# Re-packing a convolution's output through DRAM, half a super ahead of its use, in a fused convolution and two-matmul kernel

## The chip, the cores and the metric

The kernel runs on one core of one Trainium2 chip. The metric is the time of one execution in device microseconds. A profile gives the span of one execution, which is about 2 us shorter than its time.

The core's engines are named as the profile names them: PE multiplies matrices (PEld is its loading of weights), ACT, DVE and POOL work element by element, and SP here only issues DMA transfers; a q after a name is that engine's instruction queue. SBUF is the memory on the core, PSUM the one that PE writes to. To evacuate is to copy a result out of PSUM. The granted clock is the share of PE's full clock that the chip allows at that time.

## The reference, cut to what matters

```python
# x: (8, 4096, 192); weight: (8 heads, 7 taps); w_in: (192, 2048); w_out: (2048, 192)
w   = softmax(weight, axis=-1)
att = causal_conv7(x, w)          # per head of 24 channels, 7 taps back in time
h   = att @ w_in                  # 32768 tokens x 2048
g   = where(h > 0, h, exp(min(h, 0)) - 1)
out = g @ w_out                   # 32768 x 192
```

## The kernel before

Tokens go in 32 "supers" of 1024. The work of one super is:

- **conv**: two convolutions (first and second 512 tokens), each 40 small matmuls into a PSUM slot, evacuated by ACT to `csb`. In a PSUM tile each head stands in a slot of 32 partitions, of which 24 are used.
- **re-pack**: the second matmul contracts over 192 channels in three chunks of 64 partitions, twice over (two row groups of PE). SP moves the rows from the slots to `att` with 20 copies inside SBUF.
- **16 pairs**: each pair is 12 matmuls `H<-att,w_in` into one of three PSUM slots, then exp on ACT, clamp on POOL, max on DVE, giving `gT`.
- **output rounds**: 64 rounds of 4 matmuls `ops<-w_out,gT` for each half of the super, dealt out between the pairs of the *next* super, from its pair 3 (`LAG`).

The order of PE, ACT and SP comes from one list:

```python
LAG = 3; NG3 = 3
HALF_STEPS = (10, 9, 9, 9, 9, 9, 9)     # output rounds per pair, for 7 pairs
CONV_AT = (2, 10)                       # convs of super s+1 after pairs 2 and 10 of super s
...
for n in range(NP + NQ + LAG + NQ):     # n = pair number, s = super, i = pair in the super
    s, i = divmod(n, NQ)
    if n < NP: order.append(("h", n))                   # H matmuls
    if n in rounds_at: order.append(("o",) + rounds_at[n])   # output rounds
    if i in CONV_AT and s + 1 < NS and n < NP: order.append(("c", 2*(s+1) + CONV_AT.index(i)))
```

PE, in a pair: wait for `att` of the super, wait for the PSUM slot, 12 matmuls.

```python
W(s_att, 16 * NDMA_ATT * (s + 1))
wait_slot(k)
for j in range(3):
    for r in range(2):
        for c in range(2):
            pe.matmul(H[HP*c:HP*(c+1), k % 3, GS*r:GS*(r+1)],
                      w_in[HP*r:HP*(r+1), j, HP*f:HP*(f+1)],
                      att[HP*r:HP*(r+1), s % 2, j, c, :], ...)
```

SP, when both convs of a super have been evacuated:

```python
W(s_ce, m + 1)
if s >= 2: W(s_h, NQ * (s - 1))
for (hb, sl, r0, nr, j, d0) in MOVES:          # 10 moves of 8 to 24 partitions
    for r in range(2):                         # once for each row group
        sy.dma_start(att[HP*r+d0 : HP*r+d0+nr, s % 2, j, :, :],
                     csb[SLOT*sl+r0 : SLOT*sl+r0+nr, s % 2, hb, :, :]).then_inc(s_att, 16)
```

POOL, besides its clamp, issues the loads of x for three supers ahead at pair 8 of each super: one strided load of eight windows, one for the ninth, and at the start of a batch (every fourth super) a memset and a third load.

## Time and profile before

| kernel before | |
|---|---|
| time | 1244.28 us, median of 4 runs (1237.9 to 1247.79) |
| span of the profiled run | 1240.6 us |
| mean granted PE clock | 0.863 |
| time from one super to the next | 37.6 us in the mean of 28 (36.7 to 38.8) |

The page's first part gives each engine's busy time (us, share of the span, number of instructions); part 4 gives the chain of work that ended last, as shares of the span.

```profile
span 1240.6 us, 55031 instructions
PE 818.5 (66%) x25088; PEld 594.9 (48%) x25088; DVE 666.7 (54%) x1043; ACT 656.3 (53%) x1156; POOL 666.4 (54%) x1120
...
SPq 35%; PE 30%; POOL 10%; DVE 8%; ACT 6%; DMA 6%; issue 4%; ACTq 0%; DVEq 0%
SPq L447 35%; PE H L398 16%; PE ops L418 13%; DVE gT L339 7%; POOL E L237 6%; DMA att<-csb 5%; ACT E L284 3%; ACT csb L273 3%; POOL xg L201 2%; PE H L376 2%; POOL xg L202 1%; DVE Ttmp L323 1%; ACT osb L260 0%; DVE Tm L327 0%; POOL xg L192 0%
```

No engine is busy two thirds of the time, and the largest part of the chain is SP issuing DMAs (line 447, the re-pack). The waits view of the same kernel says who stood still for it (total us, number of times, longest):

```profile
POOL E L237 <- ACT E L284: 552.9, 407, 26.4
DVE gT L339 <- POOL E L237: 533.7, 257, 22.1
ACT E L284 <- PE H L398: 525.5, 407, 17.6
PE H L398 <- DMA att<-csb: 312.7, 32, 17.2
```

The first three lines are one queue: POOL waits for ACT, DVE for POOL, ACT for PE. Only the last line names a cause: 32 supers, 32 waits of PE for the re-pack, about 10 us each. The timeline of one super shows how it comes about (start us, duration us, engine, line, what, count, and in brackets the idle time before it and what ended it):

```profile
615.73 1.02 ACT L273 ACTIVATE csb<-H 128x1024 bf16<-128x1024 f32 x1 [0.47 <-PE H L376]
616.78 15.81 SPq L447 DMA_DIRECT2D att<-csb  x20
...
621.89 0.82 PE L398 MATMUL H<-att,w_in 64*64 64x512 bf16 x12
622.54 0.91 PE L418 MATMUL ops<-w_out,gT 64*64 64x192 f16 x36
...
633.98 1.50 PE L398 MATMUL H<-att,w_in 64*64 64x512 bf16 x12 [10.53 <-DMA att<-csb]
```

The second conv is evacuated at 616.75, after pair 10. SP needs 15.1 us from the first of the 20 issues to the last (which starts at 631.87), and PE goes on 2.1 us after that. PE has work only until 623.4. The first pair after the gap then takes 1.50 us instead of 0.82. The windows view of the same kernel (us, busy time and count for each engine, granted PE clock, DMA share, GB/s) shows why:

```profile
617.00:622.00 5.00, 5.00 (x192) 4.11 (x188) 3.63 (x7) 3.89 (x8) 3.56 (x6) 1.00 0.30 78
623.00:634.00 11.00, 0.47 (x28) 0.26 (x16) 2.27 (x4) 0.85 (x2) 1.43 (x3) 0.73 0.20 48
634.00:637.00 3.00, 3.00 (x52) 2.17 (x56) 0.08 (x1) 1.08 (x2) 0.80 (x2) 0.50 0.00 0
```

Before the gap the granted clock is 1.00, after it 0.50. The Trainium skill (TensorE: Matmul & The Clock Gate, Part 1) tells of a clock gate that halves the clock when PE has been idle and opens only after about 3.4 us of activity; the 3 us window at 0.50 agrees in size.

### The profile page before, as it was taken

What the parts mean: (1) busy time and instruction counts of PE and PEld (TensorE: products, weight loads), DVE (VectorE), ACT (ScalarE), POOL (GpSimd) and SP (SyncE); (2) the same over time, 40 slices, a digit from 0 to 9 for tenths busy, and PEclk for the clock granted to TensorE, in tenths of its full rate; (3) what the DMA queues carried; (4) which work ended last, traced back from release to release, by engine and by line L of the source; (5) the groups of instructions that cost most, each with busy time, mean ns of one, the idle gap of its engine ahead of it and who ended that gap; (6) DMA issues with size and microseconds to landing.
All of it is one profiled execution on the core that took longest, in us unless ns stands there. A gap on an engine that the chain in (4) does not pass through costs nothing.

```text
span 1240.6 us, 55031 instructions
## 1 busy us (share of the span) xinstructions
PE 818.5 (66%) x25088; PEld 594.9 (48%) x25088; DVE 666.7 (54%) x1043; ACT 656.3 (53%) x1156; POOL 666.4 (54%) x1120
## 2 busy tenths in 40 slices
PE   0556666766568766668766578666678566577667
PEld 0234445544446545445544455454455454455446
DVE  4555456554456545556545466454566454565553
ACT  1655456554556554556545466554566455465543
POOL 4654456554556544566544566455566544565443
PEclk9988889888888887889888898888898888898879
DMA  9221323221232212232213232213232213221111
GB/s 159 37 47 39 67 55 62 58 47 53 59 64 59 58 38 64 56 66 58 58 37 67 55 63 57 58 41 67 56 62 59 50 49 67 56 58 47 38 50 54
DMA packets 97721, 71.20 MB, mean 57 GB/s; under 512 B 52048, under 2 KB 84816, under 8 KB 97488
## 3 DMA queue, kind: packets, MB, share of 16 engines
q1 hardware_dynamic: 54928, 50.40, 14.8%
q0 software_dynamic: 42560, 17.29, 12.6%
q8 instruction: 196, 3.21, 1.1%
q14 instruction: 37, 0.30, 0.1%
HBM read 34.59 MB, written 25.17 MB: 48 GB/s over the span
## 4 chain that ended last, share of the span: by engine, by line
SPq 35%; PE 30%; POOL 10%; DVE 8%; ACT 6%; DMA 6%; issue 4%; ACTq 0%; DVEq 0%
SPq L447 35%; PE H L398 16%; PE ops L418 13%; DVE gT L339 7%; POOL E L237 6%; DMA att<-csb 5%; ACT E L284 3%; ACT csb L273 3%; POOL xg L201 2%; PE H L376 2%; POOL xg L202 1%; DVE Ttmp L323 1%; ACT osb L260 0%; DVE Tm L327 0%; POOL xg L192 0%
## 5 line engine op out<-in xcount | busy, mean ns | idle before, releaser
L339 DVE SCALAR_TENSOR_TENSOR gT<-E,H 128x512 f16<-128x512 f32 x1024 | 651.4, 683 | 552.4 <-POOL E L237 533.7
L237 POOL TENSOR_SCALAR E<-E 128x512 f32<-128x512 f32 x1024 | 606.5, 615 | 553.8 <-ACT E L284 552.9
L284 ACT ACTIVATE E<-H 128x512 f32<-128x512 f32 x1024 | 557.0, 599 | 526.3 <-PE H L398 525.5
L398 PE MATMUL H<-att,w_in 64*64 64x512 bf16 x6144 | 470.2, 414 | 353.5 <-DMA att<-csb 312.7
L418 PEld LDWEIGHTS ops<-w_out,gT 64*64 64x64 f16 x16384 | 406.4, 115 | 107.4 <-issue 33.8
L418 PE MATMUL ops<-w_out,gT 64*64 64x192 f16 x16384 | 452.3, 256 | 4.0 <-issue 2.1
L398 PEld LDWEIGHTS H<-att,w_in 64*64 64x64 bf16 x6144 | 169.5, 115 | 445.2 <-DMA att<-csb 302.4
L273 ACT ACTIVATE csb<-H 128x1024 bf16<-128x1024 f32 x64 | 66.5, 1040 | 35.7 <-PE H L376 35.7
L376 PE MATMUL H<-Tm,xg 128*24 128x122 bf16 (+3 forms) x2560 | 41.6, 211 | 60.7 <-DVE gT L339 42.6
L376 PEld LDWEIGHTS H<-Tm,xg 128*24 128x24 bf16 x2560 | 32.9, 93 | 88.9 <-DVE gT L339 56.6
L260 ACT ACTIVATE osb<-ops 128x768 f32<-128x768 f32 x64 | 52.2, 816 | 16.8 <-PE ops L418 16.4
L201 POOL DMA_DIRECT2D xg<-in_x_dram x32 | 30.1, 941 | 0.4 <-issue 0.4
L202 POOL DMA_DIRECT2D xg<-in_x_dram x32 | 18.4, 575 | 0.0
L323 DVE TENSOR_TENSOR Ttmp<-shift,wprb 128x976 bf16<-128x976 bf16 x6 | 7.0, 1175 | 0.2
L192 POOL DMA_DIRECT2D xg<-in_x_dram x8 | 4.7, 590 | 0.0
L327 DVE TENSOR_TENSOR Tm<-Tm,Ttmp 128x976 bf16<-128x976 bf16 x6 | 4.0, 667 | 0.2
L210 POOL TENSOR_SCALAR_AFFINE_SELECT shift<-shift 128x122 bf16<-128x122 bf16 x7 | 2.7, 466 | 0.0
L295 DVE MEMSET H<- 128x2048 f32 x1 | 1.8, 1765 | 1.3 <-PEq L479 1.3
L225 POOL DMA_DIRECT2D w_out<-in_moe_w_out_dram x2 | 2.2, 1102 | 0.0
L191 POOL MEMSET xg<- 6x192 bf16 x8 | 2.0, 248 | 0.0
L249 ACT ACT_TABLE_LOAD x1 | 1.3, 1283 | 0.8 <-PEq L479 0.8
L220 POOL DMA_DIRECT2D w_in<-in_moe_w_in_dram x2 | 1.3, 644 | 0.0
(14 smaller groups left out, 4.4 us busy)
## 6 DMA issues: line engine op xcount, KB each, us to landing
out_dram<-osb SPq DMA_DIRECT2D x128, 192.0 KB, 3.1
att<-csb SPq DMA_DIRECT2D x384, 48.0 KB
xg<-in_x_dram POOLq DMA_DIRECT2D x24, 384.0 KB, 5.1
att<-csb SPq DMA_DIRECT2D x128, 32.0 KB
xg<-in_x_dram POOLq DMA_DIRECT2D x8, 336.0 KB, 4.8
att<-csb SPq DMA_DIRECT2D x128, 16.0 KB
xg<-in_x_dram POOLq DMA_DIRECT2D x32, 48.0 KB, 4.6
w_in<-in_moe_w_in_dram POOLq DMA_DIRECT2D x2, 768.0 KB, 8.1
```

Source lines behind the costliest of these rows:

```text
L201: g.dma_start(xg[:, b, w0:8, :], src).then_inc(s_x[b], 16)
L202: g.dma_start(xg[:, b, 8, :], x_flat[t0 + SUP - P : t0 + SUP, :]).then_inc(s_x[b], 16)
L237: g.tensor_scalar(out=E[:, n % NE, u, :], in0=E[:, n % NE, u, :], scalar1=1.0, scalar2=0.0, op0=ALU.min, op1=ALU.max,).then_inc(s_clp)
L260: a.activation(osb[:, b, :, :, :].rearrange("p g k d -> p g (k d)"), ops[:, :, 0 : 2 * D], ACT.Copy,).then_inc(s_oev)
L273: a.activation(csb[:, s % 2, :, g, :], H[:, slot_of_conv[m] % 3, :].rearrange("p (b t) -> p b t", b=2), ACT.Copy,).then_inc(s_ce)
L284: a.activation(E[:, n % NE, u, :], H[:, k, GS * u : GS * (u + 1)], ACT.Exp).then_inc(s_exp)
L323: v.tensor_tensor(dst[:, :, :], sd, wd, ALU.mult).then_inc(s_set)
L339: v.scalar_tensor_tensor(out=gT[:, s % NG3, 2 * q + u, :], in0=E[:, n % NE, u, :], scalar=1.0, in1=H[:, slot_of_pair[n] % 3, GS * u : GS * ...
L376: ins = pe.matmul(H[SLOT * q : SLOT * q + CPH, k % 3, GS * hb + o : GS * hb + o + nc_], xg[:, s % NXB, w, CPH * h : CPH * (h + 1)], Tm[:, ...
L398: ins = pe.matmul(H[HP * c : HP * (c + 1), k % 3, GS * r : GS * (r + 1)], w_in[HP * r : HP * (r + 1), j, HP * f : HP * (f + 1)], att[HP * ...
L418: ins = pe.matmul(ops[HP * c : HP * (c + 1), g, D * kb : D * (kb + 1)], gT[HP * g : HP * (g + 1), t % NG3, f, t0 : t0 + HP], w_out[HP * g ...
L447: sy.dma_start(att[HP * r + d0 : HP * r + d0 + nr, s % 2, j, :, :], csb[SLOT * sl + r0 : SLOT * sl + r0 + nr, s % 2, hb, :, :],).then_inc( ...
```

## The change

The intent: make the re-pack cheap to issue and start it early enough to hide it. Three things are done at once.

1. **Re-pack in 8 transfers.** Each conv half is stored to a DRAM scratch (1 store), and when both have landed, 6 gathers read it back with a strided access that drops the unused slot rows. Channel order in `att` becomes "8 channels of each of 8 heads", so the rows of `w_in` are loaded in that order.
2. **Half a super ahead.** The second conv of super s+1 is done at pair 3 of super s, the first conv of super s+2 at pair 11.
3. **Output rounds earlier.** Half 0 of a super's output is accumulated inside the super, from pair 12, chunk by chunk in two blocks, as `gT` chunks appear; `gT` needs 2 buffers instead of 3.

And at the start, the weights are loaded once and copied to the other 64 partitions inside SBUF.

```diff
-NG3 = 3
-LAG = 3
+NG3 = 2
+LAG = -4
-CONV_AT = (2, 10)
+CONV_AT = ((3, 1, 1), (11, 2, 0))          # (after pair, supers ahead, which half)
...
+    bounce = nc.dram_tensor("conv_slots", (2, 2, P, SUP), BF16).ap()
-        csb = sbuf("csb", [P, 2, 2, 2, GS], BF16)
+        csb = sbuf("csb", [P, 4, 2, GS], BF16)
...
                     if r0 == 0:
-                        W(s_tt, 2 * NQ * (t + 1))
                         W(s_oev, 2 * t + half)
                     for r in range(r0, r1):
-                        kb, f = divmod(r, NF)
+                        f, kb = divmod(r, 2) if half == 0 else divmod(r, NF)[::-1]
+                        W(s_tt, 2 * NQ * t + f + 1)
...  SP, at the start
+            W(s_w, 64)
+            sy.dma_start(w_in[HP:P, :, :], w_in[0:HP, :, :]).then_inc(s_wd, 16)
+            sy.dma_start(w_out[HP:P, :, :], w_out[0:HP, :, :]).then_inc(s_wd, 16)
...  SP, at a conv
+                    W(s_ce, m + 1)
...
+                    sy.dma_start(
+                        bounce[s % 2, :, :, GS*g : GS*(g+1)].rearrange("b p t -> p b t"),
+                        csb[:, m % 4, :, :]).then_inc(s_dw[m % 4], 16)
                     if g == 0:
                         continue
+                    for k in range(m - 1, m + 1):
+                        W(s_dw[k % 4], 16 * (k // 4 + 1))
...
-                    for (hb, sl, r0, nr, j, d0) in MOVES:
-                        for r in range(2):
-                            sy.dma_start(att[...], csb[...]).then_inc(s_att, 16)
+                    for j in range(3):
+                        src = bass.AP(tensor=bounce.tensor, offset=(2*P*(s % 2) + 8*j) * SUP,
+                                      ap=[[SLOT*SUP, HEADS], [SUP, 8], [1, SUP]])
+                        for r in range(2):
+                            sy.dma_start(att[HP*r : HP*(r+1), s % 2, j, :, :], src).then_inc(s_att, 16)
```

SP waits for both stores before it issues the gathers. That is needed: the Trainium skill (DMA: Bandwidth & Descriptors, "Two DMAs through the same engine are not ordered") says that only the completion semaphore orders a DMA behind one whose bytes it reads.

## The prediction

> **What bounds the kernel now.** Not an engine: PE is busy 66%, DVE 54%, ACT 53%, POOL 54% of 1240.6 us (busy table). The chain of waits is 35% SP's queue issuing the re-pack copies (att<-csb), plus 5% their last landing. The list of waits has PE H<-att,w_in waiting 312.7 us for those copies, 32 times, about 10 us each. In the timeline, a super starts every 37-38 us (595.94, 633.98). Its second conv is evacuated at 616.75; SP then issues 20 copies until 631.8 (median 0.71 us each), the last lands 2.1 us later; PE's pair 15 had ended near 622.7. After the gap PE runs at half clock: the stretch 634-637 has a granted clock of 0.50, 12 H matmuls take 1.50 us instead of 0.82, so the first two pairs last 2.72 and 2.40 us instead of 1.39. The Trainium skill (TensorE: Matmul & The Clock Gate, Part 1) describes such a release only after about 3.4 us of activity; the trace agrees in size.
>
> **What the change does.** Per super: 20 issues become 2 stores and 6 gathers, and the conv pair is completed at pair 3 of the super before instead of pair 10. From the trace: evacuation 1.0 us, store issue 0.4 (the 128-row output stores take 0.394), landing about 3 (output stores: 3.1), then the wait for both stores, six issues of about 0.7 (the 24-row copies' figure; 64 rows of 2 KB may differ) = 4-5, last landing 2-3. Sum 11-13 us, an estimate. From pair 3 to the next super are some 13 pairs, about 19 us. So the copies leave the critical path with 6-8 us to spare, although they now go through DRAM. Gap (10 us) and slow restart (about 2.3 us) vanish.
>
> The other half of the change (output rounds 7 pairs earlier, half 0 chunk by chunk, NG3 2) does not change PE work; each round's chunk is two or more pairs old when used, so I expect no new waits there, and no gain in the loop. It shortens the tail after the last pair: about 22 us now, then about 12.
>
> **What then bounds.** The steady pair: 0.65 us H + 0.74 us output rounds on PE = 1.39 us at granted clock 1.00; DVE 2 x 0.683 = 1.37 us is nearly equal. From pair 2 to the next pair 2 without gap and ramp, read from the timeline: 1.81+1.77+1.42+5x1.39+3.21+1.50+6x1.39 = 25.0 us per super, including two conv disturbances and POOL's 1.5 us of x-load issue.
>
> **Start.** First H pair now at 37.3 us. Weights are loaded once and copied inside SBUF, but SP waits for them before its first conv store. I expect 36 us (32-42).
>
> **Sum.** 36 + 24 (first super) + 30 x 25.0 + 22.5 (last, no conv) + 12 (tail) = 844 us span; time is 2-4 us more: 847 us. Range 826 to 882. Faster by over 2%: 0.97; within 2%: 0.02; slower: 0.01.
>
> **What would show it.** PE's waits on att DMA shrink from 312.7 to under 40 us (start only); granted clock rises from 0.86 to near 1; super period 24.5-25.5 us; PE busy share over 85%, DVE near 80%; the chain consists of PE, DVE, POOL, ACT; SP re-pack below 5%.
>
> **What would make it wrong.** Gathers issuing at over 1.5 us each or landing slowly beside x loads, so that att still arrives late; a lower granted clock under unbroken load; DVE/POOL chain rather than PE setting a slower pair (27 us supers give 905); weight copies delaying the start by 10 us.

## The result, and the profile after

The changed kernel takes 870.54 us (median of 4 runs, 869.2 to 873.28). The ratio to the kernel before is 0.7003, with a 95% interval of 0.697 to 0.7037. Ratios are the mean time of one kernel's runs over that of the other's of the same rounds, so not quite the ratio of the medians quoted here. Executions over 1.5% slower than the fastest of the same kernel are left out of the means.

The page of the kernel after, the lines that answer to those above:

```profile
span 871.1 us, 54710 instructions
PE 747.2 (86%) x25088; PEld 558.8 (64%) x25088; DVE 665.7 (76%) x1043; ACT 657.0 (75%) x1156; POOL 666.6 (77%) x1120
...
PE 57%; DVE 17%; POOL 15%; ACT 4%; issue 4%; DMA 3%; SPq 0%; POOLq 0%; DVEq 0%; ACTq 0%
```

SP's queue is gone from the chain (35% before), and PE leads it with 57%. PE's busy time fell by 71 us although it does the same 25,088 matmuls, because they run at the full clock: the mean granted clock rose from 0.863 to 0.982. The waits view of the kernel after:

```profile
POOL E L245 <- ACT E L291: 188.4, 383, 31.8
ACT E L291 <- PE H L405: 181.3, 431, 19.5
DVE gT L346 <- POOL E L245: 174.5, 229, 24.9
...
PE H L405 <- DVE gT L346: 59.2, 95, 1.8
...
PE H L405 <- issue: 21.7, 3, 19.3
```

No line of PE names the re-pack any more. The one long wait (19.3 us) is at the start. The timeline of one super after:

```profile
407.52 1.07 ACT L280 ACTIVATE csb<-H 128x1024 bf16<-128x1024 f32 x1
...
408.61 0.37 SPq L453 DMA_DIRECT2D conv_slots<-csb  x1
...
411.37 3.69 SPq L470 DMA_DIRECT2D att<-conv_slots  x6
```

Conv evacuated at 408.59, store issued at once, gathers from 411.37 to 415.06. The next super's first pair comes at 426.3, so 11 us remain for the last landing, which takes some 3.7 us (the second experiment shows it).

Where the 370 us went, per super, measured between the evacuations of the first output half in successive supers: 36.7 to 38.8 us before, 25.04 to 28.4 us after, with 25.05 as the value that keeps coming back. Over 28 such intervals that is 1053.1 us against 721.8, so 331 of the 370 us. The kernel before spent 10 us of a super in the gap and about 2.3 us in the slow restart (a pair takes 1.39 us at the full clock; the two after the gap took 2.72 and 2.40 in the super that starts at 595.94, 2.72 and 2.16 in the one shown).

The prediction's span was 844 us. The measured one is 27 us longer, and two terms hold that: the first pair came at 41.06 us (36 predicted), and the 28 intervals of the loop took 721.8 us instead of 28 x 25.0 = 700. The other terms cancel.

### The profile page after: what moved, and what is told of

Read it like the earlier page. It is cut to its first block, busy times and chain, and to the rows that moved or that the text cites. A ratio compares the mean times of both kernels' runs of the same rounds, so it can differ in the third digit from the quotient of the medians.

```text
span 871.1 us, 54710 instructions
## 1 busy us (share of the span) xinstructions
PE 747.2 (86%) x25088; PEld 558.8 (64%) x25088; DVE 665.7 (76%) x1043; ACT 657.0 (75%) x1156; POOL 666.6 (77%) x1120
## 3 DMA queue, kind: packets, MB, share of 16 engines
q8 instruction: 196, 3.21, 1.6%
## 4 chain that ended last, share of the span: by engine, by line
PE 57%; DVE 17%; POOL 15%; ACT 4%; issue 4%; DMA 3%; SPq 0%; POOLq 0%; DVEq 0%; ACTq 0%
PE H L405 30%; PE ops L425 28%; DVE gT L346 17%; POOL E L245 9%; ACT E L291 4%; POOL xg L205 3%; POOL xg L206 2%; DMA w_out<-in_moe_w_out_dram 1%; DMA w_out<-w_out 1%; POOL xg L196 0%; POOL shift L214 0%; POOL w_in L224 0%; ACT osb L268 0%; POOL xg L195 0%; POOL shift L210 0%
## 5 line engine op out<-in xcount | busy, mean ns | idle before, releaser
L405 PE MATMUL H<-att,w_in 64*64 64x512 bf16 x6144 | 433.5, 381 | 81.4 <-DVE gT L346 59.2
L425 PEld LDWEIGHTS ops<-w_out,gT 64*64 64x64 f16 x16384 | 379.7, 107 | 90.5 <-issue 10.1
L425 PE MATMUL ops<-w_out,gT 64*64 64x192 f16 x16384 | 424.6, 244 | 7.0 <-issue 5.8
L405 PEld LDWEIGHTS H<-att,w_in 64*64 64x64 bf16 x6144 | 165.6, 107 | 159.6 <-DVE gT L346 86.5
L302 DVE MEMSET H<- 128x3072 f32 x1 | 2.6, 2618 | 1.5 <-PEq L504 1.5
```

Source lines behind the costliest of these rows:

```text
L405: ins = pe.matmul(H[HP * c : HP * (c + 1), k % 3, GS * r : GS * (r + 1)], w_in[HP * r : HP * (r + 1), j, HP * f : HP * (f + 1)], att[HP * ...
L425: ins = pe.matmul(ops[HP * c : HP * (c + 1), g, D * kb : D * (kb + 1)], gT[HP * g : HP * (g + 1), t % NG3, f, t0 : t0 + HP], w_out[HP * g ...
```

## The experiments

### Which part of the change closes the gap

The rival theories: (A) it matters only that the re-pack's chain fits between the second conv and the next super, so the early convs do most of the work; (B) fewer transfers, by way of DRAM, are the gain. Two kernels take the parts singly. Both keep the new output order and the new start.

**First: early convs, old copies.**

```diff
-                    sy.dma_start(bounce[...], csb[:, m % 4, :, :]) ...   # 2 stores, waits, 6 gathers
+                    for (hb, sl, r0, nr, j, d0) in MOVES:                # the 20 copies of before
+                        for r in range(2):
+                            sy.dma_start(att[HP*r+d0 : HP*r+d0+nr, s % 2, j, :, :],
+                                         csb[SLOT*sl+r0 : SLOT*sl+r0+nr, c0 : c0 + 2, hb, :])
```

> The changed kernel with its early convs and output schedule, but the old re-pack: 20 copies inside SBUF. Theory A (the gain is that the re-pack chain fits between the second conv of a super, now at pair 3, and the next super; the number of transfers only has to be small enough for that): evacuation to the next super's first pair is 17.7 us in the changed kernel's timeline (408.6 to 426.3), and the old chain needs about 15.1 us of issue plus 2.1 us of landing = 17.2 us, so it just about fits: PE waits on att copies of 0 to 1.5 us per super, time 870 to 920 us. Theory B (the gain comes from fewer transfers through DRAM): most of the old wait stays, over 1050 us.

Measured: 887.79 us, ratio 0.7157 (0.7125 to 0.719). Of the waits for the re-pack, these lines remain (PE and its weight loads, for the same copies):

```profile
PEld H L409 <- DMA att<-csb: 17.6, 17, 2.6
PE H L409 <- DMA att<-csb: 13.8, 14, 2.4
```

The 20 copies still cost SP 16.4 us per super (median of 32; 15.64 at the least), but only 14 supers of 32 make PE wait for them, about 1 us each. Theory A holds. That this kernel is 17 us slower than the changed one (11.9 us in the two profiled runs) is not these waits alone: its first pair came 1.9 us later, and the changed kernel has pauses of PE (7.6 us, counted below) that this one has not.

**Second: 8 transfers, convs as late as before.**

```diff
-CONV_AT = ((3, 1, 1), (11, 2, 0))
+CONV_AT = ((2, 1, 0), (10, 1, 1))
```

> The changed kernel with the 8 transfers through DRAM, but the convs at pairs 2 and 10 of the super before, as in the kernel before. From evacuation at pair 10: store about 0.4 + landing 3.1 + six issues 3.7 + landing 2 to 4 = 9 to 11 us, against 17.2 us before; about 6 us of pair work are left to hide it. Theory A: a wait of 3 to 5 us per super plus some cold restart, super about 30 us, time 980 to 1060 us. Theory B: close to the changed kernel, under 920 us.

Measured: 1040.44 us, ratio 0.8396 (0.8354 to 0.8439), as theory A expected. The wait and one of its gaps, from the waits view and the timeline of this run:

```profile
PE H L405 <- DMA att<-conv_slots: 147.2, 32, 19.6
...
619.36 3.69 SPq L470 DMA_DIRECT2D att<-conv_slots  x6
...
626.74 1.50 PE L405 MATMUL H<-att,w_in 64*64 64x512 bf16 x12 [4.31 <-DMA att<-conv_slots]
```

Without the start's 19.6 us the waits are 4.1 us per super. The last gather is issued by 623.05 and PE goes on at 626.74, so from the end of the last issue to PE it takes about 3.7 us, longer than the 1.4 us of the copies inside SBUF (632.59 to 633.98 in the kernel before). Even so the chain from evacuation (615.92) to PE is 10.8 us against 17.2 before.

So, against 1241 us, and with the new output order and start in all three: the early convs without the 8 transfers save 353 us, the 8 transfers without the early convs 200, both 370. They do not add, because a gap can be closed only once. The early convs alone leave a chain that nearly fits; the transfers alone leave one that does not.

### The output order

```diff
-NG3 = 2
-LAG = -4
+NG3 = 3
+LAG = 3          # and whole blocks in both halves, each after the whole super, as before
```

> The changed kernel with the old output order (whole blocks, one super plus 3 pairs behind, 3 gT buffers). My theory: the loop does not change, only the tail grows by 7 pairs' output rounds and lost overlap: 5 to 10 us more, 875 to 882 us. Rival (the chunk-by-chunk accumulation also feeds PE better in the loop): over 890 us.

Measured: 874.30 us, ratio 0.7043 (0.7021 to 0.7065). From the last H matmul's start to the end of the span the trace has 21.2 us (852.7 to 873.9), against 14.4 in the changed kernel (856.7 to 871.1) and 21.8 in the kernel before. A shorter tail is what this part buys, in one profiled run each; in the loop it buys nothing (28 intervals took 719.7 us with the old order, 721.8 with the new). In the time nothing is shown: the whole difference is 0.6%, the two ratios' intervals overlap, and 874.30 us lies just below the expected 875 to 882.

### The start

```diff
-            W(s_w, 64)                          # all weights
+            W(s_w, 48)                          # w_in only; w_out has a semaphore of its own
             sy.dma_start(w_in[HP:P, :, :], w_in[0:HP, :, :]).then_inc(s_wd, 16)
-            sy.dma_start(w_out[HP:P, :, :], w_out[0:HP, :, :]).then_inc(s_wd, 16)
...          # w_out's copy after the first six gathers, awaited before the first output round
```

> The changed kernel with w_in copied inside SBUF as soon as it has landed and w_out copied only after the first att gathers. The first pair came at 41.06 us, 5 us later than predicted. If the weight copies in front of the first conv stores cause that: first pair at 31 to 35 us, time 6 to 10 us less (861 to 865 us). If the DRAM round trip itself causes it: no change within 2 us.

Measured: 865.71 us, ratio 0.6973 (0.695 to 0.6996). The first pair came at 38.99 us: 2 us earlier, and not at 31 to 35, so the expectation was missed. The time is 4.8 us less, but the ratio's interval overlaps that of the changed kernel, and this profile has fewer pauses of PE too (2 against 8, below). The SP lines of this run's timeline show what the start still holds:

```profile
21.29 1.27 SPq L455 DMA_DIRECT2D conv_slots<-csb  x2
28.66 3.82 SPq L472 DMA_DIRECT2D att<-conv_slots  x6
32.53 0.52 SPq L480 DMA_DIRECT2D w_out<-w_out  x1
```

The stores now go out at once, but take over 6 us to land (median of the whole run 2.9), and from the last gather's issue to the first pair another 6.5 us pass. From 21.3 to 28.6 us, while the stores are under way, the windows view gives a DMA share of 1.13 (a packet is counted where it starts), with loads of w_out and x still in flight; behind the gathers come the copy of w_out, which this edit put there, and the store of the next conv. The order of the weight copies was a part of the late start only. That the other transfers in flight slow the round trip is likely from these numbers, but no run takes them away.

### Why a super takes 25.8 us and not 25.05

In the changed kernel, every super has one half of 12.19 us and one of 12.86, or 13.72 where a batch starts, and in some supers more. Three candidates: POOL's pause for the x loads (1.5 us, 2.35 at a batch start), the conv that takes one of three PSUM slots while PE has no output rounds in that pair, and pauses of PE that the profile ascribes to nothing ("issue").

**POOL's x loads spread over pairs 1, 6 and 14.**

```diff
-                if i == 8 and s + NXB < NS:
-                    load_x(s + NXB)
+                if i in (1, 6, 14) and s + NXB < NS:
+                    load_x(s + NXB, ((1, 6, 14).index(i),))    # batch start; eight windows; ninth
```

> The changed kernel with POOL's x-load issues (0.94 + 0.57 us together at pair 8, and 0.25 + 0.59 more in every fourth super) spread over pairs 1, 6 and 14. In the changed kernel's trace the half of a super without x loads lasts 12.19 us, the half with them 12.86, and 13.72 where a batch starts. If POOL's pause is what lengthens these halves, because it exceeds the slack of three PSUM slots, both become about 12.2 to 12.4, period 24.4 to 24.7, 15 to 25 us less in all (846 to 856 us). If the difference comes from something else in that half (out stores, DMA traffic), no change within 4 us.

Measured: 856.61 us, ratio 0.6919 (0.6899 to 0.6939). The half supers shrank as the first reason says: 12.86 to about 12.30, and 13.72 to about 12.57. So POOL's pause did lengthen these halves. The time is just above the expected range, because another loss grew, the pauses counted below.

**The x load at pair 14.**

```diff
-                if i == 8 and s + NXB < NS:
+                if i == 14 and s + NXB < NS:
```

> The changed kernel with the whole x load at pair 14 instead of 8, a stretch where the DMA engines were nearly idle (DMA share 0.02 against 0.9 to 1.1). The changed kernel has 4 pauses of 1.1 to 1.5 us on PE with no releaser[...]. If they are instruction fetches held up by the burst of x load, output store and conv store, they become fewer or vanish here, and the sum falls by 4 to 10 us (861 to 867 us). If they come by chance, about as many remain, and the time stays at 868 to 873 us. The pause of POOL itself stays in both cases.

Measured: 866.09 us, ratio 0.699 (0.6979 to 0.7001). The expected time came, the expected reason did not: the pauses did not become fewer (table below), and the ratio's interval lies inside that of the changed kernel. Inconclusive.

**Output rounds dealt evenly.**

```diff
-HALF_STEPS = (10, 9, 9, 9, 9, 9, 9)
+HALF_STEPS = (8, 8, 8, 8, 8, 8, 8, 8)
```

> The changed kernel with the output rounds dealt evenly, 8 per pair over all 8 pairs, instead of 10 and six times 9 with none in the conv's pair. PE then has 8 rounds (0.66 us) to do in the pair where it now waits for a slot that the conv took: the half super of 12.19 us should shrink towards the DVE's 8 x 1.37 = 10.9 us plus a remaining conv gap: period 23.8 to 24.7 us, 12 to 35 us less in all (836 to 858 us). If the evacuation between the two halves, which then has no free pair, stops PE instead, no gain or a loss.

Measured: 845.83 us, ratio 0.6828 (0.6816 to 0.684). The half supers became 11.55 and 12.38 us (13.25 at a batch start). A pair without output rounds had left PE idle while it waited for the slot that the conv held; now PE has 8 rounds there. The conv without an x load near it, and the pair after it, in the timeline of the changed kernel and then of this run:

```profile
406.18 0.63 PE L383 MATMUL H<-Tm,xg 128*24 128x98 bf16 x40
407.57 0.84 PE L405 MATMUL H<-att,w_in 64*64 64x512 bf16 x12 [0.76 <-DVE gT L346]
...
318.74 0.64 PE L383 MATMUL H<-Tm,xg 128*24 128x98 bf16 x40
319.56 0.84 PE L405 MATMUL H<-att,w_in 64*64 64x512 bf16 x12 [0.18 <-DVE gT L346]
```

This is the largest gain of a single edit to the changed kernel.

**All three (split loads, even rounds, start order).**

> The split x issues, the even rounds and the start order of the fourth run together, on the changed kernel. If the three gains add: 5 + 20 + 20 us, about 820 to 840 us. If even rounds and split loads fill the same gap: 840 to 855 us.

Measured: 845.45 us, ratio 0.6818 (0.6799 to 0.6838): no more than the even rounds alone. The pauses took up at least a part of the rest (25.4 us in this profile, 11.1 with the even rounds alone). One of them, in the timeline of this run:

```profile
253.04 0.64 PE L387 MATMUL H<-Tm,xg 128*24 128x122 bf16 x37
...
257.25 0.20 PE L387 MATMUL H<-Tm,xg 128*24 128x24 bf16 x3 [3.57 <-issue]
257.38 1.49 PE L409 MATMUL H<-att,w_in 64*64 64x512 bf16 x12
```

PE stops three matmuls before the end of a conv, which waits for nothing, and goes on 3.57 us later, at half the clock. The table counts such idle times of over 0.25 us before a PE matmul with "issue" as releaser, between 60 us from the start and 30 us before the end, read from the timelines (one profiled run each):

| kernel | pauses | us in all |
|---|---|---|
| before | 1 | 0.3 |
| changed | 8 | 7.6 |
| early convs, 20 copies in SBUF | 0 | 0 |
| late convs, 8 transfers | 0 | 0 |
| old output order | 7 | 4.8 |
| start order | 2 | 2.6 |
| split x loads | 18 | 18.7 |
| x load at pair 14 | 11 | 8.8 |
| even rounds | 13 | 11.1 |
| all three | 26 | 25.4 |
| all three, no x reload (below) | 10 | 5.0 |
| all three, no output stores (below) | 33 | 28.4 |
| even rounds, late load, start order (below) | 19 | 13.8 |
| the same with one x load (below) | 32 | 23.5 |

The sums are too small where slow pairs follow a pause; of the changed kernel's 8 pauses one had them. It ended at 447.63 and lasted 1.33 us, and that interval was 28.43 us, 3.4 us over the clean 25.05:

```profile
445.00:447.00 2.00, 0.84 (x26) 0.23 (x15) 1.82 (x4) 1.29 (x2) 1.05 (x2) 1.00 0.88 232
447.00:449.00 2.00, 1.37 (x40) 1.29 (x43) 0.00 (x0) 0.71 (x2) 0.03 (x1) 0.81 0.68 202
449.00:451.00 2.00, 2.00 (x39) 1.66 (x35) 1.28 (x2) 0.38 (x1) 1.16 (x2) 0.50 0.07 24
```

These windows of the changed kernel show the DMA engines at 0.88 of their time as the pause begins, and the granted clock at 0.50 after it.

**What the pauses need.** My guess was that PE waits for its instructions. The page lists an instruction queue among the DMA queues:

```profile
q8 instruction: 196, 3.21, 1.6%
```

That is 3.21 MB in 196 packets; divided by the 50,176 instructions of PE and PEld it is 64 B for each, an estimate that fits PE's program. If those fetches share the DMA engines with the data, taking away data traffic should take away pauses. Two kernels with a wrong result do so, both on the all-three kernel.

```diff
-                if i in LOAD_AT and s + NXB < NS:        # no x reload
+                if False:
```

> Wrong result on purpose: the all-three kernel (split x issues, even rounds, start order) without x loads after the first three supers. The all-three kernel had 12 pauses of 0.88 to 3.57 us on PE with no releaser, after the start, each with an instruction-queue packet shortly before PE went on. If these are instruction fetches that data traffic delays, taking away the x loads (about 16% of the DMA engines' span) leaves clearly fewer, under 5, and the half supers come near 11.5 us. If they are PE outrunning its own fetch whatever else the DMA engines do, about as many remain (8 or more).

```diff
+                    if t < NS - 1:                       # no output stores before the last super
+                        continue
```

> Wrong result on purpose: the all-three kernel without output stores before the last super. The same question for the stores: if data traffic of any kind delays the fetches, fewer pauses here too (under 8 of the 12); if only the x loads do, about 12 remain; if traffic has no part, about 12 in this and in the run without x reloads.

Measured in one run each, state unknown: 801.19 us without x reloads, with one pause over 0.85 us (12 with them) and half supers of mostly 11.41 us; 854.22 us without output stores, with 11 such pauses. So most of the pauses need the x loads, and none needs the output stores. By the table, the kernel with 20 copies inside SBUF has the same x loads and no pause at all. But x loads and the round trip through DRAM together are not enough either: the kernel with late convs has both and no pause, while PE waits there 4.1 us per super for the re-pack. Whether such waits give the fetches time to catch up was not tested.

That the thing delayed is an instruction fetch can be read from the kept traces, from their single records and not from a view shown here. 196 packets for 50,176 instructions are blocks of 256. Counted in the order of PE's instructions (weight loads, matmuls and semaphore instructions), all 180 pauses of the table stand at place 192 or 193 of such a block; of the changed kernel's 111 other idle times of over 0.25 us, 1 does. Each pause ends 1.1 to 1.7 us after a packet of the instruction queue has ended, and in the changed kernel that packet had started 6.2 us (median of 8) after the one before it, against 3.9 us for all packets of the loop. So PE stopped at the end of a block, and the next one was late. What makes it late in one kernel and not in another stays open, beyond the part of the x loads. The run without x reloads also loses POOL's pauses, so its 44 us are not all due to PE's.

### A version that beats both

**Even rounds, x load at pair 14, start order.**

> A candidate: even rounds, the fourth run's start order, and the whole x load at pair 14. The split loads added nothing to the even rounds and came with more pauses; the late load alone gave 4 to 5 us. If that adds to the even rounds: 835 to 842 us. If the even rounds have taken up that gain: 843 to 848 us.

Measured: 847.30 us, ratio 0.6818 (0.6798 to 0.6838). The late load gave nothing on top of the even rounds; the expected 835 to 842 us was missed.

**The same with one x load per super.** The ninth window, which started 74 rows early to end with the super, is taken with the regular stride; it reads rows past the super that nobody uses, except in the last super, which keeps its own load.

```diff
-                    ap=[[D, P], [CW * D, 8 - w0], [1, D]],
+                    ap=[[D, P], [CW * D, NW - w0], [1, D]],       # NW = 9, in the last super 8
...
+                            c0 = 0 if w == 8 and s < NS - 1 else c0
```

> The same candidate with the ninth window of x in the one strided load, so POOL issues one load per super instead of two (0.57 us less pause of POOL per super, right result). If POOL's pause beyond the slack of the PSUM slots still lengthens the half super that holds it, 0.3 to 0.6 us per super less than the third run of this call, 10 to 18 us in all. If PE's pauses have become the limit, under 5 us.

Measured: 840.20 us, ratio 0.6761 (0.6745 to 0.6778), right result: the fastest found, 3.5% under the changed kernel. The gain over the run before it is 7.1 us, between the two expectations. The half supers with the load fell from 12.58 to 12.13 us, as the shorter pause of POOL (0.57 us less) lets one expect, which would be about 13 us over the 29 supers that load x; the pauses of PE, 13.8 us before and 23.5 us in this profile, took part of it back.

## Why the prediction was right, point by point

- **Time.** Predicted 847 us (826 to 882), measured 870.54. Right within the range, 2.8% above the 847.
- **The re-pack leaves the critical path.** Right. PE's waits of 312.7 us are gone, and the chain has no SP. The estimate of the re-pack chain, 11 to 13 us against 19 available, was near: evacuation to the end of gather issue is 6.5 us (408.59 to 415.06), plus about 3.7 us of landing; 17.7 us were available (408.6 to 426.3). The experiments show that starting early is the larger part, and that the old copies, started early, would also nearly have fitted (13.8 us of waits in all), which the prediction didn't say.
- **The restart at half clock goes.** Right: mean granted clock 0.863 to 0.982. Nearly all of the rest of the clock loss is the start: from 62.6 us on, the windows view has the clock at 1.00 except in 448 to 452, after one pause (0.57).
- **The output order does not change the loop and shortens the tail.** Right, in one profiled run each: 28 intervals of 719.7 and 721.8 us; tail 21.2 and 14.4 us. Predicted was 12.
- **25.0 us per super.** The right value for a clean super (25.05 keeps coming back), but mis-sized as a mean: it was read from one super (601 to 616 and 616 to 623 of the kernel before), without a batch start and without a pause. The mean of 28 intervals is 25.8. Seven batch starts at 0.86 us are 6.0 us of the 21.8 missing; the rest are supers with pauses, slow pairs after them, and smaller delays, a loss that hardly existed in the kernel before (1 pause in its whole loop) and so could not be read from its trace.
- **36 us for the start.** Mis-sized by 5 us: 41.06. The weight copies before the first stores are part of it (38.99 without), the slow landing of stores and gathers is the rest, whose cause no run separates.
- **The predicted signs.** Super period 24.5 to 25.5 us: true of clean supers only. PE busy over 85%: 86%. DVE near 80%: 76%.

## What to carry to other kernels

When one queue's issue time stands between two stages, first ask how early its input can be ready: moving the producer half a stage ahead saved 353 of the 370 us here without making the transfers any cheaper, and cheaper transfers without it saved 200. A steady period read from one clean stretch is a lower bound; count how often the rarer stretches come (here every fourth super) and look for stalls in a loop without gaps that the loop with gaps did not have (here up to 33 pauses of PE, 1 in the kernel before). Once such a gap is closed, look at what the fullest engine does while a shared buffer is taken: eight output rounds put into the conv's pair gave another 25 us for one changed line.

## What the Trainium skill lacked or had wrong

- *TensorE: Matmul & The Clock Gate*, Part 1, ties in its table the fall of the clock to an idle window of about 3.4 us (on frequent short idle times it has a passage, without a length). Here shorter idle times had a pair at half clock after them: a wait of 2.54 us in the run with 8 late transfers (12 H matmuls in 1.50 us at 595.98), and the pause of 1.33 us in the changed kernel, with a granted clock of 0.50 in the window from 449 to 451 us. Seven other idle times of 1.3 us in the changed kernel's trace, all from 84 us on, left the clock at 1.00.
- *DMA: Bandwidth & Descriptors* has, for trn2, no issue times by the form of a transfer. The runs show, as medians on SP: 0.714 us for a copy inside SBUF of 8 to 24 partitions, 0.575 us for a gather of 64 rows of 2 KB from DRAM, 0.366 us for a store of 128 partitions. The smallest transfers took longest.
- *Runtime: NRT & Kernel Launch*, Instruction fetch mechanics, tells of instructions that come in blocks of 256 by a DMA queue, and calls the cost of crossing to the next block mostly hidden. Here it was not in every kernel: 26 pauses of PE at such a crossing, 25.4 us, in the all-three kernel, 10 and 5.0 us when the x loads were left out, none with the re-pack inside SBUF. The page does not say which other DMA traffic delays a block, and these runs settle it only for the x loads.
